# Output projection in row tiles, and one column-tile stretch per head pair, in a sigmoid-attention and token-MLP kernel

## The chip, the cores and the metric

The kernel runs on one core of a Trainium2 chip. The metric is the device time of one execution in microseconds (us), the median of the runs. Profiled times start at the first instruction; the measured time is about 2.1 us longer than the profiled span of the same run. TensorE is PE in the profile, VectorE DVE, ScalarE ACT. Ratios are the mean time of one kernel's fast runs over that of the kernel before in the same rounds on the same chip, so they are not quite the ratio of the medians that are quoted.

## The reference, cut to what matters

```python
scores = scale * q @ k.T - log(S)          # 8 batches, 12 heads, S = 448, head_dim = 64
x = sigmoid(scores) @ v                    # then heads side by side: D = 768
W = scale2 * (x @ w_q) @ (x @ w_k).T       # hidden size 64, per batch
out = relu(W.T @ x) @ w_out                # 768 x 768
```

## The kernel before

Batches go in pairs u = 0 to 3, heads in pairs j = 0 to 5: 24 pairs n = (u, j). A score couple is two matmuls in two row tiles (64 rows each, "64\*128" in the profile), followed by one sigmoid of 128x896. Transposes, values (`pv`) and the last scores are couples of column tiles ("128\*64"). The MLP of u-1 is worked off within the pairs of u: `wqk` in j=0, its transposes (`pk`), `tmp` and the mix in j=1, then 14 output chunks of six full 128x128 matmuls (`po`). Score tiles have two PSUM buffers, everything else shares four PSUM banks.

```python
        if n + 1 < N:
            tr_q(n + 1)                 # column tiles
        scores_last(n)                  # column tiles
        if n + 1 < N:
            tr_k(n + 1)
        if n >= 2:
            tr_x(n - 2)
        if u > 0 and j == 1:
            mlp_wkn(u - 1)              # pk
        scores(n, 0); scores(n, 1)      # row tiles
        whole(left)                     # output chunks, full tiles
        scores(n, 2); scores(n, 3)
        if n > 0:
            values(n - 1, 0); values(n - 1, 1)
        # ... cut: tmp in j = 1
        scores(n, 4); scores(n, 5)
        # ... cut: wqk in j = 0; in j = 1 all six mixes in a row; else whole(left - 1)

    def mlp_out(u, m, nb):
        # ... cut
        for c in range(NC):             # NC = 6
            nc.tensor.matmul(
                ps, mxs[u][c].rearrange("p b s -> p (b s)")[:, m * P : (m + 1) * P],
                wout16[:, c, nb * NB : (nb + 1) * NB],
                start=(c == 0), stop=(c == NC - 1),
            )
```

## Time and profile before

| | before |
|---|---|
| median time, 3 runs | 250.95 us (250.38 to 251.14) |
| profiled span | 248.5 us |
| PE / ACT busy | 87% / 69% |
| distance between the last scores of two pairs, u=0 | 7.21 us |
| the same, 12 / 24 output matmuls in the pair | 7.64 / 9.25 us |
| the pair with the mix | 12.25 us (12.76 in u=1) |
| last scores of the last pair to the end | 37.1 us |

The "distance between last scores" is used throughout: the time from the first last-scores matmul (128\*64, 448 wide, out to `sc`) of one pair to that of the next, read from the timeline. It is a pair's true length, whatever overlaps in it.

### The profile page before, as it was taken

How to read it: one execution, taken by the hardware profiler on the slowest of the kernel's cores; microseconds unless marked ns; L12 is line 12 of the kernel's file. 1: busy time of each engine (PE TensorE's matmuls, PEld its weight loads, DVE VectorE, ACT ScalarE, POOL GpSimd, SP SyncE). 2: the span in 40 equal slices, each digit the busy share in tenths (PEclk: the TensorE clock that was granted, in tenths of full speed). 3: DMA queues.
4: the chain of work that ended last, by engine and by line, in shares of the span. 5: the costliest groups of instructions: out<-in, count | busy, mean ns of one | idle time of the engine just before them, and what ended most of it. 6: DMA issues, size and time to landing. Idle time of an engine off the chain costs nothing.

```text
span 248.5 us, 6124 instructions
## 1 busy us (share of the span) xinstructions
PE 215.9 (87%) x2480; PEld 116.7 (47%) x2480; DVE 132.2 (53%) x230; ACT 171.7 (69%) x194; POOL 75.5 (30%) x84
## 2 busy tenths in 40 slices
PE   0878777779779999999979999999979999998992
PEld 0534334445435644545544554455444554453660
DVE  2423444454575555564685654655684564458551
ACT  2499889986677768986688678895698678724000
POOL 1655466566302131441633041343631010000000
PEclk9979999999979999999999999999999999999997
DMA  6999999999900498789872489789962543220376
GB/s 239 303 286 268 249 330 318 308 296 262 247 2 21 115 275 231 187 231 286 224 216 65 114 240 263 211 234 259 234 170 66 130 105 95 67 63 3 79 201 163
DMA packets 35387, 47.58 MB, mean 191 GB/s; under 512 B 6432, under 2 KB 31008, under 8 KB 35360
## 3 DMA queue, kind: packets, MB, share of 16 engines
q1 hardware_dynamic: 35088, 46.74, 70.2%
q8 instruction: 19, 0.31, 0.6%
q10 hardware_dynamic: 272, 0.46, 0.5%
q14 instruction: 8, 0.07, 0.1%
HBM read 36.18 MB, written 11.01 MB: 190 GB/s over the span
## 4 chain that ended last, share of the span: by engine, by line
PE 72%; ACT 17%; issue 5%; DVE 2%; DMA 2%; ACTq 0%
PE po L289 19%; PE pv L203 16%; ACT at L169 15%; PE sc L187 12%; PE ptk L155 5%; PE ptq L139 5%; PE sc L177 5%; PE px L223 4%; PE pw L236 4%; ACT mx L280 2%; PE pt L263 2%; DMA q<-in_q_dram 2%; PE pm L275 1%; DVE tmp L268 1%; PE pk L251 1%
## 5 line engine op out<-in xcount | busy, mean ns | idle before, releaser
L169 ACT ACTIVATE at<-sc,bias_t 128x896 bf16<-128x896 f32 x168 | 158.8, 1006 | 49.3 <-PE sc L177 23.7
L289 PE MATMUL po<-wout,mx 128*128 128x384 bf16 x336 | 59.6, 327 | 0.1
L187 PE MATMUL sc<-qt,kt 64*128 64x448 bf16 x288 | 47.2, 358 | 14.4 <-ACT at L169 14.0
L294 DVE COPY o<-po 128x384 f32<-128x384 f32 x56 | 31.2, 558 | 37.7 <-PE po L289 36.6
L207 DVE CAST xt<-pv 128x448 bf16<-128x448 f32 x48 | 30.0, 625 | 39.6 <-PE pv L203 36.4
L289 PEld LDWEIGHTS <-mx 128*128 128x128 bf16 x336 | 30.6, 98 | 25.2 <-issue 7.2
L203 PE MATMUL pv<-at,v 128*64 128x448 bf16 x384 | 40.9, 356 | 0.0
L116 POOL CAST q<-q 128x896 bf16<-128x896 f32 x23 | 21.5, 933 | 59.0 <-DMA q<-in_q_dram 29.9
L125 POOL CAST v<-v 128x1024 bf16<-128x1024 f32 x24 | 25.0, 1040 | 38.4 <-PE pv L203 21.0
L187 PEld LDWEIGHTS <-kt 64*128 64x128 bf16 x288 | 12.3, 93 | 43.3 <-issue 40.8
L116 POOL CAST k<-k 128x896 bf16<-128x896 f32 x24 | 22.6, 940 | 24.5 <-DMA k<-in_k_dram 16.9
L203 PEld LDWEIGHTS <-v 128*64 128x64 bf16 x384 | 19.7, 109 | 17.0 <-issue 6.1
L159 DVE COPY kt<-ptk 128x1024 bf16<-128x1024 bf16 x24 | 16.6, 690 | 9.7 <-PE ptk L155 9.7
L139 PE MATMUL ptq<-ident,q 128*64 128x128 bf16 x336 | 15.5, 238 | 6.0 <-DVE q L116 6.0
L143 DVE COPY qt<-ptq 128x896 bf16<-128x896 bf16 x24 | 15.0, 624 | 8.6 <-PE ptq L139 8.5
L139 PEld LDWEIGHTS <-q 128*64 128x64 bf16 x336 | 11.3, 119 | 14.2 <-issue 6.5
L280 ACT ACTIVATE mx<-pm 128x448 bf16<-128x448 f32 x24 | 11.7, 550 | 8.1 <-PE pm L275 8.0
L155 PEld LDWEIGHTS <-k 128*64 128x64 bf16 x336 | 15.1, 120 | 4.2 <-issue 0.8
L224 DVE COPY xn<-px 128x1024 bf16<-128x1024 bf16 x24 | 16.4, 681 | 0.4 <-PE px L223 0.4
L177 PE MATMUL sc<-qt,kt 128*64 128x448 bf16 x96 | 14.5, 382 | 2.2 <-ACT at L169 2.2
L155 PE MATMUL ptk<-ident,k 128*64 128x128 bf16 x336 | 16.4, 233 | 0.0
L279 DVE TENSOR_SCALAR mx<-pm 128x448 bf16<-128x448 f32 x24 | 13.8, 619 | 2.6 <-PE pm L275 2.4
(36 smaller groups left out, 125.5 us busy)
## 6 DMA issues: line engine op xcount, KB each, us to landing
q<-in_q_dram SPq DMA_DIRECT2D x24, 448.0 KB, 5.9
out_dram<-o SPq DMA_DIRECT2D x56, 192.0 KB, 2.7
k<-in_k_dram SPq DMA_DIRECT2D x23, 448.0 KB, 7.0
v<-in_v_dram SPq DMA_DIRECT2D x48, 128.0 KB, 6.0
v<-in_v_dram SPq DMA_DIRECT2D x48, 96.0 KB, 5.6
w<-in_moe_w_out_dram SPq DMA_DIRECT2D x6, 384.0 KB, 6.2
k<-in_k_dram ACTq DMA_DIRECT2D x1, 448.0 KB, 4.9
wqk<-in_moe_w_q_dram SPq DMA_DIRECT2D x2, 192.0 KB, 6.4
```

What stands on the lines that cost most here:

```text
L116: eng.tensor_copy(out=t16.rearrange("p b i d -> p b (i d)"), in_=ld.pop((nm, n)))
L125: nc.gpsimd.tensor_copy(out=t.rearrange("p b h s d -> p (b h s d)"), in_=v32[n % NV].rearrange("p b h s d -> p (b h s d)"),)
L139: nc.tensor.transpose(ps[HALF[b2], i].rearrange("p h n -> p (h n)"), t16[:, b2, i, :], ident16)
L155: nc.tensor.transpose(ps[HALF[b2], pos].rearrange("p h n -> p (h n)"), src, ident16)
L169: nc.scalar.activation(at, sc[:, :, 0:S], ACTF.Sigmoid, bias=bias_t, scale=attn_scale)
L177: nc.tensor.matmul(sc[HALF[b2], h, 0:S], kts[n][:, h, 3 * P + 64 * b2 : 3 * P + 64 * b2 + 64], qts[n][:, h, :], start=True, stop=True,)
L187: nc.tensor.matmul(sc[:, b2, 0:S], kts[n][HALF[b2], h, m * P : (m + 1) * P], qts[n][HALF[b2], h, :], start=True, stop=True,)
L203: nc.tensor.matmul(ps[HALF[b2]], v16s[n][:, b2, h, slot, :], rhs, start=(m == 0), stop=(m == 3))
L207: nc.vector.tensor_copy(out=t, in_=ps)
L280: nc.scalar.activation(mxs[u][c][:, 1, :], ps[1], ACTF.Relu, bias=0.0, scale=moe_scale)
L289: nc.tensor.matmul(ps, mxs[u][c].rearrange("p b s -> p (b s)")[:, m * P : (m + 1) * P], wout16[:, c, nb * NB : (nb + 1) * NB], start=(c == ...
L294: nc.vector.tensor_copy(out=ot[0][:, nb * NB : (nb + 1) * NB], in_=ps)
```

## The change

The intent is to change the tile shape of TensorE seldom. All column-tile work of a pair stands in one stretch; then come six score couples, and between them "slots" of MLP work that are row tiles too. An output slot is two 64-row matmuls side by side, one for each of two chunks. After six slots the two halves of the rows swap chunks, so that each chunk sees all 128 rows, with a drain between. The code aims at 17 slots in each pair of u=1 to 3; in the program as built a pair with output alone has 17 to 19, one with wqk 7 output slots, and two pairs of u=2 none. The mixes are spread over three pairs, in u=1 over one. Besides, there are a warm-up, split copies at the start, copies on ACT at the end, smaller pools, and PSUM banks handed out from a list. In the diffs of this document some lines are joined or shortened, and `...` stands for what is cut.

```diff
-    def mlp_out(u, m, nb):
+    def out_slot(last=False):
 ...
+        n, r = divmod(s, 12)
+        half, c = divmod(r, NC)
+        if r == 6:
+            drain()
+        for x in range(2):
+            u, m, nb = chunks[2 * n + (x ^ half)]
             nc.tensor.matmul(
-                ps, mxs[u][c]...[:, m * P : (m + 1) * P],
-                wout16[:, c, nb * NB : (nb + 1) * NB],
-                start=(c == 0), stop=(c == NC - 1),
+                state[x ^ half][1],
+                mxs[u][c]...[HALF[x], m * P : (m + 1) * P],
+                wout16[HALF[x], c, nb * NB : (nb + 1) * NB],
+                start=(r == 0), stop=(r == 11),
             )
 ...
+        drain()                                  # at a half-done group
+        if u > 0 and j == 1:
+            mlp_wkn(u - 1)
         if n + 1 < N:
             tr_q(n + 1)
-        scores_last(n)
-        if n + 1 < N:
             tr_k(n + 1)
-        ...
-        scores(n, 0) ... whole(left) ... scores(n, 3)
+        scores_last(n)
         if n > 0:
             values(n - 1, 0)
             values(n - 1, 1)
+        if n >= 2 and not (u > 0 and j == 1):
+            tr_x(n - 2)
+        mixes = ((1, (0, 1, 2, 3, 4, 5)),) if u == 1 else ((1, (0, 1)), (2, (2, 3)), (3, (4, 5)))
+        if u == 0:
+            for g in range(first, 6):
+                scores(n, g)
+            continue
+        for g in range(2, 6):
+            fill(todo, (total * (g - 1)) // 4 - (total * (g - 2)) // 4)
+            scores(n, g)
```

More of the change, by code (lines that the diff above doesn't have):

```diff
@@ L60, with bank @@
     p_qk = pool("qk", 3)
-    p_at = pool("at", 16)
+    p_at = pool("at", 15)
     p_x = pool("x", 1)
     p_one = pool("one", 1)
-    p_o = pool("o", 4)
+    p_mx = pool("mx", 2)
+    p_o = pool("o", 3)
     ps_s = pool("ps_s", 2, space=bass.MemoryType.PSUM)
-    ps_f = pool("ps_f", 4, space=bass.MemoryType.PSUM)
+    ps_f = pool("ps_f", 1, space=bass.MemoryType.PSUM)
+    free = [0, 1, 2, 3]
+    def bank(shape, dtype, name):
+        n = free.pop(0)
+        return n, ps_f.tile(shape, dtype, tag=f"f{n}", name=name)
     NV = 3
@@ L132, with tr_q @@
     qts, kts = {}, {}
-    def tr_q(n):
-        ps = ps_f.tile([P, NI, 2, NP], BF16, tag="f", name="ptq")
+    def tr_q(n, split=False):
+        fb, ps = bank([P, NI, 2, NP], BF16, "ptq")
         t16 = ld.pop(("q16", n))
@@ L142, in tr_q, with evac, tr_k @@
         t = p_qk.tile([P, 2, S], BF16, tag="qt", name="qt")
-        nc.vector.tensor_copy(
-            out=t.rearrange("p h (i n) -> p h i n", i=NI), in_=ps.rearrange("p i h n -> p h i n")
-        )
-        qts[n] = t
-    def tr_k(n):
-        ps = ps_f.tile([P, 8, 2, NP], BF16, tag="f", name="ptk")
+        def evac(hs):
+            nc.vector.tensor_copy(
+                out=t[:, hs].rearrange("p h (i n) -> p h i n", i=NI),
+                in_=ps[:, :, hs, :].rearrange("p i h n -> p h i n"),
+            )
+        qts[n] = t
+        free.append(fb)
+        if split:
+            return evac
+        evac(slice(0, 2))
+    def tr_k(n, split=False):
+        fb, ps = bank([P, 8, 2, NP], BF16, "ptk")
         t16 = ld.pop(("k16", n))
@@ L158, in tr_k, with evac @@
         t = p_qk.tile([P, 2, 4 * P], BF16, tag="kt", name="kt")
-        nc.vector.tensor_copy(
-            out=t.rearrange("p h (s n) -> p h s n", s=8), in_=ps.rearrange("p s h n -> p h s n")
-        )
+        def evac(hs):
+            nc.vector.tensor_copy(
+                out=t[:, hs].rearrange("p h (s n) -> p h s n", s=8),
+                in_=ps[:, :, hs, :].rearrange("p s h n -> p h s n"),
+            )
         kts[n] = t
+        free.append(fb)
+        if split:
+            return evac
+        evac(slice(0, 2))
     ats = {}
@@ L197, in values @@
         u, j = pairs[n]
-        ps = ps_f.tile([P, S], F32, tag="f", name="pv")
+        fb, ps = bank([P, S], F32, "pv")
         for m in range(4):
@@ L207, in values @@
         nc.vector.tensor_copy(out=t, in_=ps)
+        free.append(fb)
         xts[u, 2 * j + h] = t
@@ L216, in tr_x @@
             xns[u] = p_x.tile([P, 4, 2, D], BF16, tag="xn", name="xn")
-        ps = ps_f.tile([P, 4, 2, 2, HD], BF16, tag="f", name="px")
+        fb, ps = bank([P, 4, 2, 2, HD], BF16, "px")
         for h in range(2):
@@ L227, in tr_x, with mlp_wqk @@
         )
+        free.append(fb)
     wqk, wkn, tmps, mxs = {}, {}, {}, {}
-    def mlp_wqk(u):
-        ps = [ps_f.tile([P, S], F32, tag="f", name="pw") for _ in range(2)]
-        for h in range(H):
-            for b2 in range(2):
-                nc.tensor.matmul(
-                    ps[b2], wqk16[HALF[b2], h, :], xts[u, h][HALF[b2]],
-                    start=(h == 0), stop=(h == H - 1),
-                )
-        wqk[u] = [p_one.tile([P, S], BF16, tag=f"wqk{b2}", name="wqk") for b2 in range(2)]
-        for b2 in range(2):
-            nc.vector.tensor_copy(out=wqk[u][b2], in_=ps[b2])
+    pw = {}
+    def mlp_wqk(u, h):
+        if h == 0:
+            pw[0], pw[1] = [bank([P, S], F32, "pw") for _ in range(2)]
+        for b2 in range(2):
+            nc.tensor.matmul(
+                pw[b2][1], wqk16[HALF[b2], h, :], xts[u, h][HALF[b2]],
+                start=(h == 0), stop=(h == H - 1),
+            )
+        if h == H - 1:
+            wqk[u] = [p_one.tile([P, S], BF16, tag=f"wqk{b2}", name="wqk") for b2 in range(2)]
+            for b2 in range(2):
+                if b2 and u == NU - 1:
+                    nc.scalar.copy(out=wqk[u][b2], in_=pw[b2][1])
+                else:
+                    nc.vector.tensor_copy(out=wqk[u][b2], in_=pw[b2][1])
+                free.append(pw[b2][0])
     def mlp_wkn(u):
-        ps = ps_f.tile([P, 4, 2, P], BF16, tag="f", name="pk")
+        fb, ps = bank([P, 4, 2, P], BF16, "pk")
         for b2 in range(2):
@@ L255, in mlp_wkn @@
         )
+        free.append(fb)
     def mlp_tmp(u):
@@ L259, in mlp_tmp @@
         for nb in range(2):
-            ps = ps_f.tile([P, NB], F32, tag="f", name="pt")
+            fb, ps = bank([P, NB], F32, "pt")
             for m in range(4):
@@ L267, in mlp_tmp @@
                     )
-            nc.vector.tensor_copy(out=tmps[u][:, nb * NB : (nb + 1) * NB], in_=ps)
-    def mlp_mix(u, c):
-        if c == 0:
-            mxs[u] = [p_one.tile([P, 2, S], BF16, tag=f"mx{n}", name="mx") for n in range(NC)]
-        ps = [ps_f.tile([P, S], F32, tag="f", name="pm") for _ in range(2)]
-        for b2 in range(2):
+            dst = tmps[u][:, nb * NB : (nb + 1) * NB]
+            if nb and u == NU - 1:
+                nc.scalar.copy(out=dst, in_=ps)
+            else:
+                nc.vector.tensor_copy(out=dst, in_=ps)
@@ new lines, in mlp_tmp, with relu, mlp_mix @@
+            free.append(fb)
+    def relu(dst, ps, act):
+        if act:
+            nc.scalar.activation(dst, ps, ACTF.Relu, bias=0.0, scale=moe_scale)
+        else:
+            nc.vector.tensor_scalar(dst, ps, moe_scale, 0.0, ALU.mult, ALU.max)
+    def mlp_mix(u, c, b2s=(0, 1), act=None):
+        if u not in mxs:
+            mxs[u] = [p_mx.tile([P, 2, S], BF16, tag=f"mx{n}", name="mx") for n in range(NC)]
+        got = []
+        for b2 in b2s:
+            fb, ps = bank([P, S], F32, "pm")
@@ L275, in mlp_mix @@
             nc.tensor.matmul(
-                ps[b2], tmps[u][HALF[b2], c * P : (c + 1) * P], wqk[u][b2][HALF[b2]],
+                ps, tmps[u][HALF[b2], c * P : (c + 1) * P], wqk[u][b2][HALF[b2]],
                 start=True, stop=True,
             )
-        nc.vector.tensor_scalar(mxs[u][c][:, 0, :], ps[0], moe_scale, 0.0, ALU.mult, ALU.max)
-        nc.scalar.activation(mxs[u][c][:, 1, :], ps[1], ACTF.Relu, bias=0.0, scale=moe_scale)
-    ot = {}
-    def mlp_out(u, m, nb):
-        if nb == 0:
-            ot[0] = p_o.tile([P, D], F32, tag="o", name="o")
-        ps = ps_f.tile([P, NB], F32, tag="f", name="po")
-        for c in range(NC):
+            got.append((b2, fb, ps))
@@ new lines, in mlp_mix, with drain @@
+        for b2, fb, ps in got:
+            relu(mxs[u][c][:, b2, :], ps, b2 if act is None else act)
+            free.append(fb)
+    chunks = []
+    state = {}
+    pos = [0]
+    drained = [False]
+    ot = {}
+    def drain():
+        if pos[0] % 12 == 6 and not drained[0]:
+            nc.tensor.drain()
+            drained[0] = True
+    def out_slot(last=False):
+        s = pos[0]
+        if s >= NC * len(chunks):
+            return False
+        n, r = divmod(s, 12)
+        half, c = divmod(r, NC)
+        if r == 0:
+            for x in range(2):
+                state[x] = bank([P, NB], F32, "po")
+        if r == 6:
+            drain()
+            drained[0] = False
+        for x in range(2):
+            u, m, nb = chunks[2 * n + (x ^ half)]
@@ L289, in mlp_out @@
             nc.tensor.matmul(
-                ps, mxs[u][c].rearrange("p b s -> p (b s)")[:, m * P : (m + 1) * P],
-                wout16[:, c, nb * NB : (nb + 1) * NB],
-                start=(c == 0), stop=(c == NC - 1),
-            )
-        nc.vector.tensor_copy(out=ot[0][:, nb * NB : (nb + 1) * NB], in_=ps)
-        if nb == 1:
+                state[x ^ half][1],
+                mxs[u][c].rearrange("p b s -> p (b s)")[HALF[x], m * P : (m + 1) * P],
+                wout16[HALF[x], c, nb * NB : (nb + 1) * NB],
@@ L296, in mlp_out @@
+                start=(r == 0), stop=(r == 11),
+            )
+        pos[0] += 1
+        if r == 11:
+            u, m, _ = chunks[2 * n]
+            o = p_o.tile([P, D], F32, tag="o", name="o")
             for x in range(2):
-                b2, i = divmod(2 * m + x, NI)
-                nc.sync.dma_start(
+                fb, ps = state.pop(x)
+                dst = o[:, x * NB : (x + 1) * NB]
+                if last and x:
+                    nc.scalar.copy(out=dst, in_=ps)
+                else:
+                    nc.vector.tensor_copy(out=dst, in_=ps)
+                free.append(fb)
+            for y in range(2):
+                b2, i = divmod(2 * m + y, NI)
+                eng = nc.scalar if last and y else nc.sync
+                eng.dma_start(
@@ L299, in mlp_out @@
                     out=out[2 * u + b2].rearrange("(p i) d -> p i d", i=NI)[:, i, :],
-                    in_=ot[0][HALF[x]],
+                    in_=o[HALF[y]],
                 )
-    def outs_of(u):
-        return [(u, m, nb) for m in range(NI) for nb in range(2)]
+        return True
     w32 = {}
@@ L334 @@
     nc.vector.tensor_copy(out=ident16, in_=ident)
+    fb, ps = bank([P, P], F32, "pwarm")
+    for _ in range(36):
+        nc.tensor.matmul(ps, ident16, ident16, start=True, stop=True)
+    free.append(fb)
     for t in v32:
@@ L342 @@
     cast1(0, "q", nc.vector)
-    cast1(0, "k", nc.gpsimd)
-    tr_q(0)
-    tr_k(0)
+    k0 = ld.pop(("k", 0))
+    k016 = p_c16.tile([P, 2, NI, HD], BF16, tag="k16", name="k16")
+    nc.gpsimd.tensor_copy(out=k016[:, 0].rearrange("p i d -> p (i d)"), in_=k0[:, 0])
+    nc.scalar.copy(out=k016[:, 1].rearrange("p i d -> p (i d)"), in_=k0[:, 1])
+    ld["k16", 0] = k016
+    eq = tr_q(0, split=True)
+    eq(slice(0, 1))
+    ek = tr_k(0, split=True)
+    for hs in (slice(0, 1), slice(1, 2)):
+        ek(hs)
+        if hs.start == 0:
+            eq(slice(1, 2))
     cast1(1, "q", nc.gpsimd)
@@ L348, with fill @@
     cast_v(0)
-    outs = []
-    def whole(segs_left):
-        take = -(-len(outs) // segs_left) if outs else 0
-        for _ in range(take):
-            mlp_out(*outs.pop(0))
+    SLOTS = 17
+    def fill(todo, n):
+        for _ in range(n):
+            if todo and todo[0] is not None:
+                todo.pop(0)()
+            else:
+                if todo:
+                    todo.pop(0)
+                out_slot()
     for n, (u, j) in enumerate(pairs):
@@ L379 @@
                 nc.gpsimd.tensor_copy(out=wout16[:, c, :], in_=w32[c])
-        left = {0: 2, 1: 1}.get(j, 2 * (NJ - j) + (2 if u < NU - 1 else 0))
+        drain()
+        first = 0
+        if n == 0:
+            scores(n, 0)
+            scores(n, 1)
+            first = 2
+        if u > 0 and j == 1:
+            mlp_wkn(u - 1)
         if n + 1 < N:
             tr_q(n + 1)
+            tr_k(n + 1)
         scores_last(n)
-        if n + 1 < N:
-            tr_k(n + 1)
-        if n >= 2:
+        if u > 0 and j == 1:
             tr_x(n - 2)
-        if u > 0 and j == 1:
-            mlp_wkn(u - 1)
-        scores(n, 0)
-        scores(n, 1)
-        whole(left)
-        scores(n, 2)
-        scores(n, 3)
         if n > 0:
@@ L399 @@
             values(n - 1, 1)
+        if n >= 2 and not (u > 0 and j == 1):
+            tr_x(n - 2)
         if u > 0 and j == 1:
             mlp_tmp(u - 1)
-        scores(n, 4)
-        scores(n, 5)
+        todo = []
         if u > 0 and j == 0:
-            mlp_wqk(u - 1)
-        elif u > 0 and j == 1:
-            for c in range(NC):
-                mlp_mix(u - 1, c)
-            outs += outs_of(u - 1)
-        else:
-            whole(left - 1)
+            todo = [None] * (SLOTS - H) + [lambda h=h: mlp_wqk(u - 1, h) for h in range(H)]
+        mixes = ((1, (0, 1, 2, 3, 4, 5)),) if u == 1 else ((1, (0, 1)), (2, (2, 3)), (3, (4, 5)))
+        for jj, cs in mixes:
+            if u > 0 and j == jj:
+                todo = [None] * 4
+                for c in cs:
+                    todo += [lambda c=c: mlp_mix(u - 1, c)] + [None] * (12 // len(cs) - 1)
+                if cs[-1] == NC - 1:
+                    todo.append(lambda: chunks.extend((u - 1, m, nb) for m in range(NI) for nb in range(2)))
+        if u == 0:
+            for g in range(first, 6):
+                scores(n, g)
+            continue
+        scores(n, 0)
+        scores(n, 1)
+        outs = SLOTS - sum(t is not None for t in todo)
+        end = (pos[0] + outs) % 12
+        outs += 6 - end if 4 <= end <= 8 else 0
+        total = outs + sum(t is not None for t in todo)
+        for g in range(2, 6):
+            fill(todo, (total * (g - 1)) // 4 - (total * (g - 2)) // 4)
+            scores(n, g)
+        while todo:
+            t = todo.pop(0)
+            if t is not None:
+                t()
+    U = NU - 1
+    while out_slot(last=True):
+        pass
+    tr_x(N - 2)
+    for h in range(H - 2):
+        mlp_wqk(U, h)
     values(N - 1, 0)
     values(N - 1, 1)
-    tr_x(N - 2)
-    mlp_wqk(NU - 1)
+    mlp_wqk(U, H - 2)
+    mlp_wqk(U, H - 1)
     tr_x(N - 1)
-    mlp_wkn(NU - 1)
-    mlp_tmp(NU - 1)
+    mlp_wkn(U)
+    mlp_tmp(U)
     for c in range(NC):
-        mlp_mix(NU - 1, c)
-    for args in outs + outs_of(NU - 1):
-        mlp_out(*args)
+        mlp_mix(U, c, (0,), act=c % 2)
+    chunks.extend((U, m, nb) for m in range(NI) for nb in range(2))
+    for c in range(NC):
+        out_slot(last=True)
+        mlp_mix(U, c, (1,), act=c % 2)
+    while out_slot(last=True):
+        pass
 _INS = ['q', 'k', 'v', 'moe_w_q', 'moe_w_k', 'moe_w_out']
```

## The prediction

> **What bounds the kernel now.** I read the page's busy table first, then the 40 slices, then the TensorE (PE) timeline of one ordinary head pair, the ScalarE (ACT) timeline of the same stretch, and the windows that the clock rows point to. The time is the profiled span (248.5 us) plus about 2.4 us.
>
> ```profile
> PE 215.9 (87%) x2480; PEld 116.7 (47%) x2480; DVE 132.2 (53%) x230; ACT 171.7 (69%) x194; POOL 75.5 (30%) x84
> PE   0878777779779999999979999999979999998992
> ACT  2499889986677768986688678895698678724000
> PEclk9979999999979999999999999999999999999997
> ```
>
> The reader sees two regimes. In slices 2 to 9 (batch pair u=0, no MLP work yet) ACT is at 8 to 9 tenths and PE at 7: the sigmoids set the pace. From slice 13 on PE is at 9 and sets it; the last slices have PE alone. PE's clock fell twice, in slices 2 and 12.
>
> One pair with 12 output matmuls, and ACT just before it:
>
> ```profile
> 154.91 0.58 PE L139 MATMUL ptq<-ident,q 128*64 128x128 bf16 x14
> 155.33 0.55 PE L177 MATMUL sc<-qt,kt 128*64 128x448 bf16 x4
> 155.71 0.55 PE L155 MATMUL ptk<-ident,k 128*64 128x128 bf16 x13
> ...
> 156.70 0.70 PE L187 MATMUL sc<-qt,kt 64*128 64x448 bf16 x4
> 157.33 1.15 PE L289 MATMUL po<-wout,mx 128*128 128x384 bf16 x6
> 158.42 0.36 PE L187 MATMUL sc<-qt,kt 64*128 64x448 bf16 x2
> 159.06 0.37 PE L187 MATMUL sc<-qt,kt 64*128 64x448 bf16 x2 [0.28 <-ACT at L169]
> 159.36 1.70 PE L203 MATMUL pv<-at,v 128*64 128x448 bf16 x16
> 161.00 0.55 PE L187 MATMUL sc<-qt,kt 64*128 64x448 bf16 x4
> 161.48 1.15 PE L289 MATMUL po<-wout,mx 128*128 128x384 bf16 x6
> ```
>
> ```profile
> 149.46 3.70 ACT L169 ACTIVATE at<-sc,bias_t 128x896 bf16<-128x896 f32 x4
> ```
>
> The shapes 128*64 (columns), 64*128 (rows) and 128*128 (full) alternate: seven changes in a pair. From the starts in this trace: two column or row tiles run together, 4 ns apart; such a couple costs 0.187 us at 448 columns and 0.056 us for a transpose; a full matmul of 384 costs 0.163 us. At a change the next start comes about 0.29 us after a 448-wide matmul, so a change costs 0.10 us. Four sigmoids take 3.70 us, so their cadence is (3.70 - 1.01)/3 = 0.90 us. A score couple's start is 0.41 us before its sigmoid's; its buffer is free again 0.05 us after the sigmoid's end.
>
> **What the Trainium skill says.** "TensorEngine Tiling (Array Packing)", Tiling Modes, says that changing the tiling mode drains TensorE; the 0.10 us per change agrees. The same page, Restrictions and Gotchas, says that different row tiles can't be in one PSUM bank at once: this is why the new output, whose halves swap banks at half of the sum, needs a drain. No run here shows that drain's cost. "TensorE: Matmul & The Clock Gate", Single matmul latency, gives (398 + N)/2.4 ns, 326 ns for N = 384; the trace has 326. From it I estimate the drain: the next matmul waits 326 ns instead of 163, plus a restart, so 0.20 us. Part 1 of that page says that the clock is halved after an idle window of about 3.4 us. The windows show the same, and that a half-busy one is enough:
>
> ```profile
> 10.40:13.81 3.41, 1.49 (x14) 0.45 (x11) 0.69 (x1) 3.19 (x5) 2.29 (x3) 1.00 1.10 312
> 13.81:17.22 3.41, 3.06 (x34) 1.84 (x35) 0.62 (x1) 2.92 (x4) 2.25 (x3) 0.50 1.06 312
> 24.05:27.46 3.41, 2.14 (x33) 1.01 (x29) 1.29 (x2) 3.35 (x5) 1.88 (x2) 1.00 1.24 172
> 68.42:71.84 3.42, 2.26 (x13) 0.69 (x14) 2.51 (x5) 3.04 (x5) 0.00 (x0) 1.00 0.01 3
> 71.84:75.25 3.41, 3.33 (x38) 2.12 (x38) 2.14 (x4) 2.08 (x5) 0.93 (x1) 0.50 0.00 0
> ```
>
> The first two numbers are the window's length and PE's busy time, and the third from the end is the granted clock. PE busy 1.49 us, four score couples, was followed by a window at 0.50. So was 2.26 us with single 64-row matmuls, while 2.14 us with a full mix was not. The edge lies near there.
>
> **The change, part by part.** I call the column-tile stretch C and the row-tile stretch R.
>
> C: ptq 0.42, ptk 0.45, last scores 0.38, pv 1.54, px 0.45, change 0.10: 3.32 us. If an output group is left open across it (it is in most pairs), only two PSUM banks remain for five tiles, and pv and px wait for VectorE (DVE) copies of 0.62 and 0.69 us: 0.15 us more.
>
> R without output: the first sigmoid starts at 0.41 and ends at 1.41; the third score couple starts at 1.47, the fourth at 2.36, then every 0.90: the sixth at 4.15, column work at 4.43. So a pair of u=0 takes 4.43 + 3.32 = 7.75 us, where the distance between last scores is 7.21 now, because pv and the transposes no longer lie between score couples. Four such distances: +2.2. The head saves 1.0 (36 warm-up matmuls, copies in halves): **+1.2 us**.
>
> R with 18 slots (a slot is two 64-row matmuls side by side, so 0.163 us as before): 1.47 to the third couple (four slots fill 1.03 of it), three more couples with 14 slots 0.57 + 2.28, change 0.28, drain 0.20: 4.8. With C 3.47 and the drain at the boundary 0.1 that is 8.4 us; with 17 slots 8.2. Before, 24 matmuls take 9.25 and 12 take 7.64, mean 8.45 for 18. So five changes saved (0.5 us) pay for little but the wait at the third couple (0.43), the drains and the banks.
>
> Spreading the mix is worth more. Now the pair after wqk takes 12.25, with PE waiting for relus. But the transposes of wqk now open the next column stretch, right after wqk's end, and wait for two DVE copies (0.62 each): I find 9.9 for j=0 (8.83 now) and 10.2 for j=1. Net per u -1.0. Adding the pairs: u=1 53.7 against 56.0 us, u=2 53.6 against 54.9, u=3 up to its last pair 45.7 against 48.4: **-6.3 us**.
>
> The order of the built program tells the rest. Of the 252 output slots of u=0 to 2 the loop places 203: two pairs of u=2 (j=2, 3) have none, since their chunks come only at the end of j=3. So 49 slots, 49 x 0.163 = 8.0 us, come after the last scores, with four drains (0.8). The tail's middle is as long as before (about 8.5 us up to the first mix). The last 84 slots gain 1.8 by early starts and lose eight drains (1.6); the end gains 0.5 by two copies and two queues; the last pair is longer by 1.3 with 17 slots instead of 12, less the 6 matmuls (1.0) that stood after it: **+8.8 us** with 0.5 for bank waits.
>
> Clock: R of u=0 holds six couples in 4.4 us, 26% of it. A 3.41 us window that has over 2.7 us of R falls below the edge; by the lengths that happens in about 0.7 of each such pair, and the half clock then costs C about 1.3 us. Five pairs of u=0, two of u=2 and the mix pair of u=1 (which has one now): 4.4 + 1.9 + 0.5, about **+6.8**; not measured here, so I count 4.
>
> Sum: 250.95 + 1.2 - 6.3 + 8.8 + 4 = 258.65, rounded to 258.5.
>
> **The rivals.** (1) PE stays full: each of 18 pairs takes its own work, 3.32 + 1.14 + 17 x 0.163 + 0.10 = 7.3 us, plus 5 us for wqk's transposes and tmp: 137 against 159, and with the tail some 240 us. For it: PE is at 9 tenths, and the changes are real. Against it: two score buffers and 0.90 us per sigmoid make the sixth couple wait until 4.15 us whatever PE has, and ACT's own 7 x 0.90 = 6.3 us per pair can't be hidden in C. (2) Gain and backlog cancel, with cheap drains (0.05) and no clock loss: 251 to 253. For it: u=0 windows of 2.14 us keep the clock today. (3) The clock falls in nearly every sparse pair and drains cost 0.3: 264 us.
>
> **Range and chances.** Rivals 2 and 3 are most of my range; rival 1 needs most of my waits to be wrong. A kernel with so fine a slot plan was probably tuned on a chip, which speaks for rival 1 and widens the lower side. 247 to 267; faster 0.13, same 0.29, slower 0.58.
>
> **What would show it.** Right: distances between last scores of 7.7 or more in u=0 and 8.2 to 8.5 in pairs with 17 to 18 slots; waits of the third score couple for a sigmoid; the first wqk transposes waiting over 1 us for DVE; half-clock windows in u=0 and in u=2's two empty pairs; an output block of 8 us before the last wqk; 0.36 us between the starts on both sides of a drain. Wrong: pairs near 7.3 us, no half-clock window after 20 us, or row-tile output couples further apart than 0.17 us (their weight loads not hidden).

## The result, and the profile after

The changed kernel takes **270.51 us** (268.67 to 272.05, 4 runs) against 251.04 us; the ratio of the fast runs is 1.0765 (1.0676 to 1.0853). It is slower, as forecast, but by 19.5 us instead of 7.5, and outside the stated range. Executions over 1.5% slower than the fastest of the same kernel are left out of the means. The result is correct.

The page of the changed kernel, busy shares and slices:

```profile
span 269.3 us, 6921 instructions
PE 227.0 (84%) x2852; PEld 132.8 (49%) x2852; DVE 124.1 (46%) x218; ACT 177.2 (66%) x209; POOL 75.3 (28%) x84
...
PE   7678668768869999999878699999889999998992
ACT  3766785886397788777587867883877888214320
PEclk9975997989988999999997989999999999999997
```

PE's clock row falls in eight slices instead of two (the last slice, where nothing runs, not counted), four of them in u=0, and ACT's row there is no longer a plain 8 or 9. A pair of u=0 on the PE timeline (start, length, instruction, what ended the idle time before it):

```profile
38.44 0.37 PE L209 MATMUL sc<-qt,kt 64*128 64x448 bf16 x2 [0.53 <-ACT at L191]
39.34 0.36 PE L209 MATMUL sc<-qt,kt 64*128 64x448 bf16 x2 [0.53 <-ACT at L191]
40.23 0.37 PE L209 MATMUL sc<-qt,kt 64*128 64x448 bf16 x2 [0.53 <-ACT at L191]
40.53 0.58 PE L147 MATMUL ptq<-ident,q 128*64 128x128 bf16 x14
...
41.52 0.96 PE L199 MATMUL sc<-qt,kt 128*64 128x448 bf16 x4
42.27 2.86 PE L225 MATMUL pv<-at,v 128*64 128x448 bf16 x16
```

PE does a couple every 0.90 us and idles between; then the column stretch runs slow: the sixteen values matmuls take 2.86 us, where they took 1.70 before. The windows of the trace (bounds, length, PE busy time, ..., third from the end the granted clock):

```profile
37.82:41.24 3.42, 1.82 (x34) 1.00 (x33) 0.09 (x1) 3.42 (x5) 1.64 (x3) 1.00 1.11 239
41.24:44.65 3.41, 3.41 (x30) 1.90 (x26) 1.85 (x3) 1.75 (x2) 2.47 (x4) 0.50 1.04 356
150.46:153.88 3.42, 1.76 (x23) 0.74 (x21) 1.25 (x2) 3.42 (x6) 0.98 (x1) 1.00 0.46 93
153.88:157.29 3.41, 3.41 (x40) 2.23 (x36) 1.32 (x2) 2.54 (x3) 1.81 (x2) 0.50 0.03 7
```

A window with PE busy 1.8 us is followed by one at half clock, in u=0 and again in the pairs of u=2 that have no output slots. A pair with 17 slots, from its first score couples on:

```profile
93.05 0.55 PE L209 MATMUL sc<-qt,kt 64*128 64x448 bf16 x4
93.44 0.81 PE L355 MATMUL po<-wout,mx 64*128 64x384 bf16 x8
94.58 0.36 PE L209 MATMUL sc<-qt,kt 64*128 64x448 bf16 x2 [0.32 <-ACT at L191]
...
96.85 0.99 PE L355 MATMUL po<-wout,mx 64*128 64x384 bf16 x10
```

The third score couple waits for a sigmoid, as worked out. And the chain of work that ended last, behind the last scores (each "issue" piece is at a drain):

```profile
228.29 0.08 issue
228.37 2.13 PE po L355 x24
230.50 0.08 issue
230.57 2.13 PE po L355 x24
...
245.39 1.70 DVE mx L310 x3
247.13 0.36 PE pm L318
...
250.05 2.13 PE po L355 x24
```

Twelve slots take 2.13 us and their drain 0.08 more, 2.2 us, where twelve times 0.163 is 1.96. So a drain costs 0.25 us; the starts on its two sides are 0.41 us apart.

Where the 20.8 us between the two profiled spans are (from the last scores of the pairs named):

| stretch | before | after | difference | predicted |
|---|---|---|---|---|
| start to pair 6 (u=0) | 52.1 | 59.0 | +7.0 | 1.2, and 2.6 of clock |
| pair 6 to pair 23 (u=1 to 3) | 159.3 | 160.5 | +1.2 | -6.3, and 1.4 of clock |
| pair 23 to the end | 37.1 | 49.7 | +12.6 | +8.8 |

The prediction counted 4 us of clock for the whole; it is split here as its own 4.4 to 2.4.

### The profile page after: what moved, and what is told of

The parts are those of the page before. It is cut to its first block, busy times and chain, and to the rows that moved or that the text cites. A ratio compares the mean times of both kernels' runs of the same rounds, so it can differ in the third digit from the quotient of the medians.

```text
span 269.3 us, 6921 instructions
## 1 busy us (share of the span) xinstructions
PE 227.0 (84%) x2852; PEld 132.8 (49%) x2852; DVE 124.1 (46%) x218; ACT 177.2 (66%) x209; POOL 75.3 (28%) x84
## 3 DMA queue, kind: packets, MB, share of 16 engines
q10 hardware_dynamic: 1232, 2.82, 2.7%
## 4 chain that ended last, share of the span: by engine, by line
PE 70%; ACT 17%; issue 7%; DVE 4%; POOL 0%; ACTq 0%; POOLq 0%; DVEq 0%
PE po L355 17%; PE pv L225 16%; ACT at L191 15%; PE sc L209 9%; PE ptk L170 5%; PE ptq L147 5%; PE sc L199 4%; PE px L246 4%; PE pw L261 4%; PE pt L294 2%; ACT mx L308 2%; PE pm L318 2%; DVE wqk L271 2%; PE pwarm L413 1%; DVE mx L310 1%
## 5 line engine op out<-in xcount | busy, mean ns | idle before, releaser
L355 PE MATMUL po<-wout,mx 64*128 64x384 bf16 x672 | 70.5, 323 | 3.0 <-ACT mx L308 0.6
L355 PEld LDWEIGHTS <-mx 64*128 64x128 bf16 x672 | 33.6, 94 | 32.4 <-issue 14.7
L225 PE MATMUL pv<-at,v 128*64 128x448 bf16 x384 | 46.9, 392 | 0.0
L209 PEld LDWEIGHTS <-kt 64*128 64x128 bf16 x288 | 16.2, 94 | 51.5 <-issue 43.7
L371 DVE COPY o<-po 128x384 f32<-128x384 f32 x44 | 23.0, 554 | 37.9 <-PE po L355 37.9
L153 DVE COPY qt<-ptq 128x896 bf16<-128x896 bf16 (+1 forms) x25 | 15.1, 605 | 45.3 <-PE ptq L147 45.3
L225 PEld LDWEIGHTS <-v 128*64 128x64 bf16 x384 | 26.6, 124 | 18.1 <-issue 8.7
L176 DVE COPY kt<-ptk 128x1024 bf16<-128x1024 bf16 (+1 forms) x25 | 16.6, 664 | 1.9 <-PE ptk L170 1.5
L369 ACT COPY o<-po 128x384 f32<-128x384 f32 x12 | 5.7, 478 | 17.2 <-PE po L355 17.2
L246 PEld LDWEIGHTS <-xt 128*64 128x64 bf16 x336 | 13.4, 110 | 4.8 <-issue 2.6
```

What stands on the lines that cost most here:

```text
L209: nc.tensor.matmul(sc[:, b2, 0:S], kts[n][HALF[b2], h, m * P : (m + 1) * P], qts[n][HALF[b2], h, :], start=True, stop=True,)
L225: nc.tensor.matmul(ps[HALF[b2]], v16s[n][:, b2, h, slot, :], rhs, start=(m == 0), stop=(m == 3))
L246: nc.tensor.transpose(ps[HALF[par], m, :, h, :], src, ident16)
L355: nc.tensor.matmul(state[x ^ half][1], mxs[u][c].rearrange("p b s -> p (b s)")[HALF[x], m * P : (m + 1) * P], wout16[HALF[x], c, nb * NB : ...
L371: nc.vector.tensor_copy(out=dst, in_=ps)
```

## The experiments

Eleven experiments ran, all with correct results. In the texts on record, "the kernel before" of each job has its own median, between 250.6 and 251.3 us.

### Dummy matmuls in the sparse row stretches

```diff
+    def filler(n):                     # two banks of the pool, never read
+        for _ in range(4):
+            for x in range(2):
+                nc.tensor.matmul(got[x][1], kts[n][HALF[x], 0, 0:P], qts[n][HALF[x], 0, 0:NB], ...)
             for g in range(first, 6):
+                if g >= 2:
+                    filler(n)
                 scores(n, g)
```

> Edit: in the changed kernel, dummy row-tile matmuls (4 couples, 0.65 us) before the third to sixth score couple, in the pairs of u=0 and the two pairs of u=2 without output slots; nothing else. Theory CLOCK (the sparse row stretch lets the granted clock drop to half for windows of 3.41 us, and the column stretch then runs slow): the half-clock windows of these pairs vanish (now at 20.76, 24.17, 41.24, 58.30, 143.64 and 153.88 us; those at 13.93 and 78.78 us may stay), the distances between last scores in u=0 go from 9.60, 7.94, 9.36, 8.16 (35.1 us) to 7.75 each (31.0), the two pairs of u=2 from 9.6 each to 8.4; the time falls from 270.5 by 6 to 9 us, to about 263, although the kernel has more work. Rival WAITS (these pairs are long because of waits for sigmoids and copies, the clock is a symptom): distances stay over 8.5 and the time is 270 or more.

Measured: **263.67 us** (262.91 to 264.35), ratio 1.0478. More work made the kernel 6.8 us faster. In its trace the only half-clock window before the end is the one behind the mix of u=1 (71.65 to 75.06). The four distances in u=0 are 7.82, 7.81, 7.81, 7.81. Its windows at the like places (columns as above):

```profile
17.04:20.45 3.41, 3.15 (x37) 1.78 (x34) 0.00 (x0) 3.41 (x5) 1.66 (x2) 1.00 1.07 297
37.52:40.93 3.41, 3.35 (x48) 1.97 (x45) 2.54 (x5) 2.10 (x3) 1.76 (x3) 1.00 1.10 278
```

PE is busy for over 3.1 us of the window and keeps its clock. The clock theory holds, also in size, and the rival WAITS falls: nothing but dummies was added, and the pairs got shorter. One detail missed: the two pairs of u=2 went to 9.33 and 9.31, not 8.4. The dummies themselves cost time there: a mix waits 0.63 us for a relu on ACT (at 144.44 us), and in the code dummies and mixes take their banks from the same four. The first of these pairs without dummies and at full clock stands in the next run, whose code is the same there; its distance is 8.45 us:

```profile
128.07 0.57 PE L199 MATMUL sc<-qt,kt 128*64 128x448 bf16 x4
...
136.52 0.57 PE L199 MATMUL sc<-qt,kt 128*64 128x448 bf16 x4
```

### The old order in u=0

```diff
+        if u == 0 and n > 0:
+            tr_q(n + 1); scores_last(n); tr_k(n + 1)
+            if n >= 2:
+                tr_x(n - 2)
+            for g in range(4):
+                scores(n, g)
+            values(n - 1, 0); values(n - 1, 1)
+            scores(n, 4); scores(n, 5)
+            continue
```

> Edit: in the changed kernel, the pairs 1 to 5 of u=0 get the order of the kernel before (last scores between the transposes of q and k, pv between the fourth and fifth score couple); nothing else. Theory SEPARATION (taking pv and the transposes out from between the score couples both lengthens the pair to 7.75 us and makes the row stretch so sparse that the clock drops): distances of u=0 return to 7.21 us with no half-clock window between 20 and 58 us; the four distances sum to 28.9 instead of 35.1, and the first one gains too: the time falls by 6 to 8 us, to about 263.5. Rival HEAD (the loss in u=0 comes from the new start, the smaller pools or the fixed banks): distances stay over 7.6 and the time within 2 us of 270.5.

Measured: **261.20 us** (260.67 to 262.48), ratio 1.0388: a gain of 9.3 us, more than the 6 to 8 expected; in the traces 8.1 of it are in u=0, and 1.3 in the pair behind it, which had a half-clock window too (10.61 us, now 9.32). Distances in u=0 are 7.28, 7.27, 7.27, 7.27, with no half-clock window between 17.3 and 68.5 us. The last scores of pair 6 come at 50.95 us, against 59.04 in the changed kernel and 52.85 with the dummies. So of the 8.1 us that separation costs in u=0 in these traces, 6.2 are the clock and 1.9 the longer pairs (with their dummies). The rival HEAD falls: the new start is all there in this run, and pair 6 is 1.1 us earlier than in the kernel before.

### All mixes in one pair

```diff
-        mixes = ((1, (0, 1, 2, 3, 4, 5)),) if u == 1 else ((1, (0, 1)), (2, (2, 3)), (3, (4, 5)))
+        mixes = ((1, (0, 1, 2, 3, 4, 5)),)
```

> Edit: in the changed kernel, all six mixes of every u in pair j=1 (as it does for u=1), so that the output chunks are there two pairs earlier in u=2 and u=3; nothing else. Theory BACKLOG (two pairs of u=2 have no output slots, so 49 slots move behind the last scores): the output block before the last wqk falls from 49 to 13 slots (9.1 us to about 2.6), the half-clock windows at 143 and 154 us vanish (2.4 us), the pairs j=1 of u=2 and u=3 grow by 1 to 1.5 us each, and the two pairs of u=2, now with 16 to 18 slots, stay near 8.4: time down by 5 to 7 us, to about 264.5. Rival SAME WORK (output work costs its 0.163 us per slot wherever it stands): within 1.5 us of 270.5.

Measured: **267.17 us** (265.46 to 269.52), ratio 1.0595; the profiled run is the slowest of four, so only lengths that don't hang on u=0 are taken from it. From the last scores of pair 23 to the end it has 43.2 us instead of 49.7: the 36 slots did leave the tail, and they cost little in the pairs that took them, 8.25 to 8.79 us. But the mix pairs of u=2 and u=3 grew to 14.35 and 14.26 us from 10.22 and 11.41, with a half-clock window each. Time fell by 3.3 us (3.6 by its fast runs) instead of 5 to 7: BACKLOG is right on the tail, and the burst of mixes gives half of it back.

### Full tiles behind the last scores

```diff
+            for c in range(NC):
+                nc.tensor.matmul(ps, mxs[u][c]...[:, m * P : (m + 1) * P],
+                    wout16[:, c, x * NB : (x + 1) * NB], start=(c == 0), stop=(c == NC - 1))
 ...
-    while out_slot(last=True):
-        pass
+    rest()                             # the open group, then full 128x128 chunks
```

> Edit: in the changed kernel, behind the last scores the output uses full 128x128 matmuls without drains, but for the group already open and the one between the mixes; 10 drains fewer, the rest unchanged. Theory DRAIN (a drain in row tiles puts 0.41 us between the starts on its two sides instead of 0.163: 0.25 us each, exposed in the tail): time down by 2.5 us less 0.2 for two more tile changes, to 268.2. Rival HIDDEN (the copies out of PSUM set the tail's pace anyway): within 0.7 us of 270.5.

Measured: **267.44 us** (265.94 to 269.93), ratio 1.0626. The last stretch is 46.9 us instead of 49.7. DRAIN holds: ten drains less are 2.8 us less.

### The transposes of wqk later

```diff
-        if u > 0 and j == 1:
-            mlp_wkn(u - 1)
         if n + 1 < N:
             tr_q(n + 1)
 ...
             tr_x(n - 2)
+            mlp_wkn(u - 1)
```

> Edit: on top of e2_u0_old_order (261.2 us; taken as the base because u=0 is quiet in it), the transposes of wqk stand behind px instead of at the head of the column stretch. Theory COPIES (at the head they wait for two DVE copies of 0.62 us that start only when wqk ends, so the distance j=0 to j=1 is 9.98 us where its work is worth 8.5): the distances 12 to 13 and 18 to 19 fall from 9.98 to 8.4 to 8.6, that of 6 to 7 from 9.3 to about 8; the next distances grow by at most 0.7 each: time down by 2 to 4 us, to about 258. Rival BANKS (two free PSUM banks and the chain of DVE copies set this column stretch whatever the order): what the first distance gains the second loses, time within 1 us of 261.2.

Measured: **261.67 us** (259.39 to 264.23), ratio 1.0383 against 1.0388 of its base: the same. The undisturbed two distances of u=3 went from 9.98 and 11.41 to 9.04 and 12.17, a sum of 21.2 instead of 21.4; those of u=1 from a sum of 21.4 to 20.5. So BANKS holds in u=3: what the first distance gains the second loses. That it is the chain of DVE copies that passes the wait on was not tested alone.

### Full tiles in every slot

```diff
-        for x in range(2):             # two 64-row matmuls, swapped at r == 6 behind a drain
+        x, c = divmod(r, NC)           # one 128-row matmul, one bank at a time, no drain
```

> Edit: on top of e2_u0_old_order, every output slot is one full 128x128 matmul (one bank, no swap, no drain) in the same places: the row-tile form alone is undone. Per pair with slots this brings back 8 changes of tile (0.8 us at 0.10 each) and takes away one to two drains (0.25 in a row stretch, 0.18 at its end) and one held bank (0.15); behind the last scores it takes away 12 drains (3.0 us). Theory LITTLE (the row tiles' gain is about what their drains cost): pairs with 17 or 18 slots go from 8.44 and 8.79 to 8.6 to 9.0, the tail shortens by 3: time 259 to 263.5. Rival INTENT (keeping one tile shape is worth 0.5 us and more per pair net of drains): 264.5 or more.

Measured: median **259.57 us** of six runs (254.92 to 261.27); three of them count as fast (254.92, 256.18, 258.72), ratio 1.0222. Against its base (1.0388) that is 4 us better by the fast runs and 1.6 us by the medians; the three fast runs are those with the highest granted clock (0.955 to 0.986, the others 0.943 to 0.950), so the size is not sure, but INTENT falls. The profile is of a run counted as slow; its pairs with slots, outside half-clock windows, have 8.44, 8.76 and 8.44 us, and the base 8.44, 8.79 and 8.44. In the first of these the row stretch is 0.25 us longer (6.01 against 5.76, with 0.1 less of it a wait for a sigmoid), and the column stretch 0.25 shorter (2.43 against 2.68). So eight changes of tile a pair cost no more there than drains and a held bank.

### The warm-up alone, on the kernel before

```diff
     nc.vector.tensor_copy(out=ident16, in_=ident)
+    ps = ps_f.tile([P, P], F32, tag="f", name="pwarm")
+    for _ in range(36):
+        nc.tensor.matmul(ps, ident16, ident16, start=True, stop=True)
```

> Edit: the kernel before, with the 36 warm-up matmuls of the change and nothing else. Theory: the first transposes and scores, slow from 6 to 10 us now, run at the full clock, the last scores of pair 0 come about 1 us earlier (8.68 now); loads of k then hold pair 1, so that 0.3 to 1.2 us is left at the end: 250 to 250.8 against 251.3. Rival: the loads alone set the start, 251.3.

Measured: 251.89 us (249.95 to 252.43), ratio 1.0022 (0.9985 to 1.0058): the same. The last scores of pair 0 come at 7.96 instead of 8.68 us, then three half-clock windows (12.58 to 22.82 us) take it back: pair 2 comes at 24.39 instead of 23.22. Neither text had that. In this trace warming early without work to follow brought more cold windows, not fewer; that the warm-up is their cause is not shown, since the kernel before has runs at the same clock (0.969) too.

### The mix spread, on the kernel before

```diff
         scores(n, 0)
+        if u > 0 and j == 2:
+            mlp_mix(u - 1, 3)
         scores(n, 1)
+        if u > 0 and j == 2:
+            mlp_mix(u - 1, 4)
 ...
         scores(n, 4)
+        if u > 0 and j == 1:
+            mlp_mix(u - 1, 0); mlp_mix(u - 1, 1)
```

> Edit: the kernel before, with only the spreading of the MLP mix: three of six mixes stay in pair j=1 (two of them before its last score couple), three go between the first score couples of pair j=2, and the output starts there after them. Theory BURST (the six mixes in a row let PE wait for relus on ACT and DVE, about 2.5 us per u, so that this pair takes 12.25 to 12.76 us): that pair falls to about 10.3, the next one grows by about 1, and the half-clock window at 72 us vanishes: time down by 2.5 to 5 us, to 246.5 to 249. Rival ACT (the relus only push the sigmoids back, the sum of the two pairs stays): within 1 us of 251.3.

Measured: **249.12 us** (248.66 to 249.35), ratio 0.9923 (0.9895 to 0.9950). That is 1.9 us, less than the 2.5 to 5 expected. The mix pair falls to 10.06 us as expected, but 12 output matmuls move from j=2 to j=4, which goes from 7.64 to 9.25, while j=2 stays long, 9.63. BURST names a true wait; most of it is replaced by ACT, which then runs without a gap in j=2. By stretches, u=2 gains 0.2 us and u=3 with the tail nothing, as the rival ACT said; 1.3 us are gained in u=1, where the half-clock window of 71.84 us is gone. So what is left is nearly all the clock.

### The repairs together

```diff
             fill(todo, (total * (g - 1)) // 4 - (total * (g - 2)) // 4)
+            if n in (7, 14, 15):
+                filler(n)              # and the edits of e2 and e4
```

> Edit: the changed kernel with the repairs together: the old order in u=0 (as in e2), full tiles without drains behind the last scores (as in e4), and dummy row-tile matmuls in the three other sparse pairs (the mix pair of u=1 and the two pairs of u=2 without slots). Theory SUM (separation in u=0, half clock in sparse pairs and drains are separate and add up): from the 261.2 of e2, 3.0 for the drains, 1.4 for the u=2 pairs and 1.2 for the pair behind the mix of u=1: 255 to 256.5; no half-clock window after 20 us; what is left against 251 is the output moved behind the last scores. Rival OVERLAP (the repairs hit the same time): 258 or more.

Measured: 260.68 us (259.91 to 262.37), ratio 1.0385. This run failed as a test: the dummies between the mixes wait for the relus to free banks (0.66 us at 67.32, 0.51 at 69.90), all that stands behind them on PE waits with them, and that pair went from 12.12 to 16.73 us. Without those 4.6 us it would stand at 256.1, which is inside SUM, but that is arithmetic and not a run. The next one leaves the dummies out.

### Old order in u=0, old tail

```diff
     for c in range(NC):
-        mlp_mix(U, c, (0,), act=c % 2)
+        mlp_mix(U, c)
     chunks.extend(...)
-    for c in range(NC):
-        out_slot(last=True)
-        mlp_mix(U, c, (1,), act=c % 2)
     rest()
```

> Edit: the changed kernel with the old order in u=0 (as e2) and, behind the last scores, full tiles without drains (as e4) and all twelve mixes of the last u before the first output, as in the kernel before; no dummy matmuls (those between the mixes cost e9 4.6 us: that pair took 16.73 instead of 12.12). Theory SUM: from e2's 261.2, 2.7 to 3.0 for the drains (e9's tail from the last scores on was 47.0 us against 49.8), and 2 to 2.5 for the mixes (from the first mix to the last matmul 19.5 us in the changed kernel, 17.0 in the kernel before): 255.5 to 257; what then remains of the tail against before is the block of 49 slots, about 8 us. Rival NOISE OF THE CLOCK (e2's gain and the tail overlap): 258.5 or more.

Measured: **257.97 us** (257.24 to 259.98), ratio 1.0298: between SUM and its rival. The expectation counted something twice: the 19.5 us from the first mix to the last matmul hold seven drains, 1.74 us, and six of them (1.5 us) were in the other term already. The two blocks of its tail on the PE timeline:

```profile
217.14 7.97 PE L553 MATMUL po<-wout,mx 128*128 128x384 bf16 x48
...
236.95 13.81 PE L553 MATMUL po<-wout,mx 128*128 128x384 bf16 x84 [0.17 <-DVE mx L310]
```

The last 84 matmuls take 13.81 us, just what the kernel before needs. What is left of the loss can be read off: the first block, 7.97 us, which that kernel has inside its pairs. By stretches against before: u=0 -0.7, pairs 6 to 23 -1.2, the last stretch 46.0 against 37.1, +8.9; the sum is, but for rounding, the difference of the spans, 255.4 to 248.5.

### A version that beats both

The spread mix of e8 and the warm-up of e7 are in it, and:

```diff
+        if n < 2:
+            filler(n)                  # three dummy couples between the score couples of pairs 0 and 1
-        nc.scalar.activation(mxs[u][c][:, 1, :], ps[1], ACTF.Relu, ...)
+        if c >= 4 and u < NU - 1:      # both relus of the last two mixes on DVE
+            nc.vector.tensor_scalar(mxs[u][c][:, 1, :], ps[1], moe_scale, 0.0, ALU.mult, ALU.max)
 ...
+            if b2 and u == NU - 1:     # and one wqk and one tmp copy of the last u on ACT
+                nc.scalar.copy(out=wqk[u][b2], in_=ps[b2])
```

> Edit: the kernel before with the parts that the runs so far say are worth something: the mix spread over two pairs as in e8 (249.1), with the relus of the last two mixes all on DVE, since ACT ran without a gap there; the 36 warm-up matmuls together with dummy matmuls between the score couples of pairs 0 and 1, which keep the clock from dropping there (it dropped after the warm-up alone); of the last u, one wqk copy and one tmp copy on ACT and the last store on a second queue. Theory: e8's 1.9 us, about 1.6 us at the start (last scores of pair 2 at 21.6 us, as with the dummies in e1, instead of 23.2), about 1 us at the end, 0.5 to 1 us for the relus: 245 to 247, faster than both kernels. Rival: the start is held by loads and the relus only move to DVE: 248.5 to 249.5.

Measured: **245.89 us** (245.61 to 247.57), ratio 0.9809 (0.9772 to 0.9847): 1.9% faster than the kernel before, with an interval clear of 1, and some 9% faster than the changed one. From its trace: no half-clock window from 5.85 us to the end, the last scores of pair 2 at 21.92 us (23.22 before), and 9.09 us in j=2 (9.63 with the mix spread alone, 9.26 in the kernel before).

## Why the prediction was right or wrong

The direction was right, the size was not: 258.5 forecast, 270.5 measured, above the upper end of 267. Nearest was rival 3, which still fell 6.5 us short; rival 1, a PE that stays full, is refuted.

**Right.** The row stretch without output is paced by the sigmoids: 7.75 us was worked out for a pair of u=0, 7.81 stands in the run whose clock stays up. Up to pair 6 that run is 0.8 us behind the kernel before, where the prediction said +1.2. The distances with 17 and 18 slots were forecast as 8.2 and 8.4; with 17 it is 8.44, and with 18 at full clock 8.39 (j=4 of u=2 in the run with dummies; 8.60 in u=1 of the changed kernel has the end of a half-clock window in it, and the pair of 8.79 has 19 slots). Couples of row-tile output start 0.163 us apart, so their weight loads are hidden. The wait at the third score couple, the DVE copies ahead of `pk` (9.9 forecast, 9.98 measured), the 49 slots behind the last scores (8.8 us with their drains, 9.1 measured) and the half-clock windows in the named pairs are there.

By the spans the forecast is 13.1 us short (20.8 against 7.7). Three terms of the sum failed: the clock by about 6.6 us, the tail by 3.8 and the pairs by 3.1; the length of u=0 apart from its clock came out 0.4 us better. (The small sums are right but for rounding: the parts of C add up to 3.34 and not 3.32, those of the tail to 8.9 and not 8.8.)

**Wrong, the clock.** The step that failed is "about +6.8; not measured here, so I count 4". The mechanism was right, and the undiscounted term was too small already. The dummies bring 6.8 us by the medians, but they cost 0.9 us in each of two pairs of u=2, and leave the window behind the mix of u=1; that 6.8 comes out again is luck. In the profiled run, which is 0.9 us above the median, the half clock cost 6.2 us in u=0 (4.4 in the prediction), 1.3 in j=0 of u=1 (10.61 us against 9.29), 0.2 in j=2 of u=1, and about 2.9 in u=2 (9.01, 9.60 and 9.59 us, against 8.44, 8.44 and 8.39 at full clock; the second of these is taken to be like the first): an estimate of 10.6 in all. The discount was no working; it stood for doubt, and doubt belongs into the range. The edge that was read off the windows of before (1.49 us busy falls, 2.14 doesn't) held in this kernel: in u=0 and u=2, windows at full clock with PE busy 1.67 to 1.82 us were followed by half clock, and two with 1.90 and 1.91 were not. It is not sharp: 1.83 us in e3 (38.94 to 42.35) kept the clock, and 2.23 us with single mix matmuls in e5 (121.92 to 125.34) lost it. And the same code of j=2 in u=2 has a half-clock window here and none in e2 and e11, where the windows lie at other places in it.

**Wrong, the pairs.** The -6.3 us in all: measured is +1.2, of which about 4.4 are the half clock just counted. The rest is 3.1: without the half clock u=1 takes 55.5 us where 53.7 was worked out, u=2 53.9 for 53.6, and u=3 46.7 for 45.7. In u=3 it is the mix pair, 11.41 us instead of 10.2; it has 15 output slots beside two mixes, that of u=2 has six and takes 10.22. So "Net per u -1.0" held in u=2 (-0.9) and failed in u=3 (+0.3). In u=1 the mixes stand in one pair, of 12.13 us, for which the prediction shows no figure; there the cause stays open but for the pairs with 17 slots, 0.2 us longer each, in part since a drain costs 0.25 us and not 0.20, and one at a stretch's end 0.18 and not 0.1. On the kernel before, spreading the mix gained nothing in u=3 and 0.2 us in u=2 either: what PE no longer waits for in j=1 it waits for in the next pairs.

**Wrong, the tail.** +8.8 forecast, +12.6 measured. "The last 84 slots gain 1.8 by early starts" is the step: from the first mix to the last matmul the changed kernel needs 19.5 us and the one before 17.0. In place of the gain of 0.2 net there is a loss of 2.5: 1.7 for seven drains, and 0.7 because the interleaved mixes wait for relus one by one (the run with the old tail brings both back). The middle took 0.7 more and not the same, and the end gained nothing by two queues and two copies (4.8 us in both), where 0.5 was counted.

**Where the expected gain went.** The change does save the changes of tile. But run with full tiles in every slot, its own plan is no slower (259.57 against 261.20 us). And in e11, where the clock of u=0 and the drains behind the last scores are repaired, the stretch from pair 6 to pair 23 is only 1.2 us shorter than before, while it does 54 fewer output slots (186 against 240), worth 8.8 us; half-clock windows that are still in it cost an estimated 2 us (9.31, 9.19 and 8.76 us in three pairs, against 8.39 to 8.44 at full clock). PE's time was moved behind the last scores, not saved. Two pairs of u=2 have no slots, because the spread mixes finish late: with all mixes in one pair (e3) the last stretch fell from 49.7 to 43.2 us, though the mix pairs grew. Not settled: how much of a boundary drain is the swap's and how much the change of tile that lies at the same place.

## What to carry to other kernels

Before grouping work by kind, look at what fills the gaps of the engine that sets the pace: pv and transposes between the score couples kept the sigmoids fed, and kept TensorE busy enough for its clock. Lay the 3.41 us windows of the clock over a new schedule and count PE's busy time in each; a term that follows from that belongs in the sum in full. Where the windows will lie, and so which of them fall, differed from run to run here: that part is for the range. And work that goes to where nothing runs beside it has not been hidden but added: count what is left at the end of the loop.

## What the Trainium skill lacked or had wrong

- "TensorE: Matmul & The Clock Gate", Part 1, gives an idle window of about 3.4 us as what brings the half clock; further down it also tells of a kernel whose frequent short idle times did so, but gives no busy share. Here half-busy windows were enough: with PE busy 1.67 to 1.82 us of 3.41 in the sparse pairs, and 1.91 and 2.26 us where single 64-row matmuls of the mix stood among them, half clock followed; at 1.90 and 1.91 us with column tiles among them it did not. From half clock, a window with PE busy 2.84 us was followed by another one at half clock, and those with 3.06 and 3.41 us by full clock; but full clock also followed 2.82 us (e11) and half clock 3.04 us (e9), so the busy time that the profile shows does not decide alone. Warm-up matmuls that no work followed brought nothing (ratio 1.0022).
- "TensorEngine Tiling (Array Packing)", Tiling Modes and Restrictions and Gotchas, says that a change of mode drains TensorE, and that software must keep row tiles out of one PSUM bank, and gives no cost for either: a change took 0.10 us between back-to-back matmuls, an explicit drain between the row tiles 0.25 us (0.41 between starts instead of 0.163).
